# S4's convolution over 8 blocks of 256 samples, by the transforms of even and odd samples, in a kernel that runs it beside eight dense experts

## The chip, the cores and the metric

One core of one Trainium2 chip runs the whole kernel. The metric is the device time of one execution in microseconds, the median of three runs. TensorE multiplies matrices, VectorE and ScalarE work on elements, GpSimd (POOL) issues the accumulating DMAs here, and SyncE (SP) issues nearly all other DMAs, in the order in which the program lists them.

## The reference

For u of 2048 tokens and 512 channels, with xn the layer norm of u, the output is the sum of three branches:

```
xn  = layernorm(u)
out = u + A(xn) + B(xn)
A:  K[d, l] = Re sum_n C[d, n] * exp(dt[d] * A[d, n] * l) * dt[d] * B[d, n]      l = 0 .. 2047, n = 0 .. 127
    y[l, d] = sum_j K[d, j] * xn[l - j, d] + xn[l, d] * Dskip[d]                  (by FFTs of length 4096)
B:  sum over all 8 experts e of softmax(xn @ w_gate)[e] * (silu(xn @ w1[e]) @ w2[e])      w1: 512 x 1792, w2: 1792 x 512
```

All eight experts take part for every token, so branch B is dense. Branch A is called S4 here.

## The kernel before, in words

**The experts.** The outer loops run over 8 experts e, 4 blocks tb of 512 tokens and 4 groups d of w1's rows (two pairs of 128 each in the first three groups, one pair in the last). Every fp32 operand is split into a high and a low fp16 half, and a product is three matmuls. `product` (line 1371) makes the first layer into three PSUM tiles hb by seven products instead of eight (a Strassen-like scheme whose sums of weights and of tokens, w1s and xop, are made beforehand), in matmuls of 256 columns. `pop` (lines 1354 to 1356) makes the second layer y in matmuls of 512 columns. `block` lists it in four slots per group: a product, a copy between hb's tiles on ScalarE (lines 1605, 1615, 1600), activations (1387, 1391), then `slot`, which pops some units of the second layer, splits weights of the next expert, and lets S4 go on. The low half of an activation is made on VectorE (1400). The token sums xop are loaded anew for each block (line 1596, SP). The first block (`plain`, line 1662) is made without the scheme, while the inputs come in.

**S4.** It goes by 32 chunks c of 16 channels. Its state basis is made for two chunks at once (`s4_basis`). `s4_tables` makes powers by doubling on VectorE. `s4_kernel` contracts them on TensorE to K (kgen, 64 fp32 matmuls), and `s4_kernel_out` copies that to ksb on ScalarE and turns it through DRAM (kd) into kt, 128 positions by 16 blocks for each channel. `s4_kf` and `s4_uf` transform the blocks of K and of xn: 128-point transforms at half-odd frequencies as matmuls with dfth, 6 of 256 columns each. `s4_conv` then makes, frequency by frequency, the convolution over the 16 blocks as a complex product in three real ones, m = 0 to 15, on VectorE (lines 884, 889, 890), with its sums in lines 869 to 874, 897, 898. `s4_back` transforms back (yp, 6 matmuls of 256 columns) and `s4_out` scales into ysb and stores to ys4. All S4 results on TensorE, the transposes and the scale totals share one PSUM bank, tag "s4": `take_bank` evacuates what is there before the next takes it.

**What sets the order.** The order of each engine's instructions is written out when the program is made, by a planner. `bg_run`, once per slot, lets S4's VectorE steps go on as far as a budget allows, 0.92 of TensorE's time in the slot less VectorE's other work, by the modelled cost that each step yields. S4's products are one per slot at most: `s4_pe` lists for each c, in this order, kf(c), back(c-1), kernel(c+2), uf(c+1), each when `until` says that its operands' step was listed two slots before and the bank is free. `s4_dve(c)` lists the tables of c+2 and then the conv of c. Before the last block, `bg_until("s4")` lists what is left of S4; in that block `s4_final` adds ys4 to the output.

**Buffers that the steps below name.** ksb and ysb have one buffer each; kt one; s4raw two; the tables' temporaries are ta and tt. `load_rest` (lines 144 to 148) puts four small loads on SP's queue ahead of the next weights (493) and of the stores of xn to DRAM (`x0_send`, 307).

Of the kernel before, what the change touches and what calls it, by code (L numbers as in the profile page):

```python
# [18 lines left out]
P = 128  # L19
# [7 lines left out]
MULTS = (1, 128, 2, 256, 4, 512, 8, 1024, 16, 32, 64)  # L27
NK = len(MULTS)
XSH = 8
# [4 lines left out]
def s4_moe_kernel(  # L34
# [29 lines left out]
    NI = NT  # L64
    DQS = [(0, 1), (2, 3), (4, 5), (6,)]
# [318 lines left out]
    def gates_squares(row):  # L384
        gsq = sb.tile([P, KT * E], F32, tag="s4p1", bufs=1, name="gsq")
        S.activation(gsq, wgt.rearrange("p k e -> p (k e)"), AF.Square, accum_out=row)

    def gates_split():
# [3 lines left out]
        wgf = sb.tile([P, 6, E], F32, tag="s4p2", bufs=1, name="wgf")  # L392
# [265 lines left out]
    ZSH = 18  # L658

    def s4_dft_load():  # L660
        s4["dft"] = sb.tile([P, 4, P], F32, tag="tb", name="dft", bufs=1)
        nc.sync.dma_start(s4["dft"], dft)

    def s4_dft():

        dftt = s4["dft"]
        times(dftt[:, 2:4, :], dftt[:, 2:4, :], DSH)
        V.tensor_copy(dfth[:, 0], dftt)
        V.tensor_tensor(dfth[:, 1], dftt, dfth[:, 0], op=ALU.subtract)
# [6 lines left out]
    upad = cp.tile([P, 2, DC, NI + 1], F32, name="upad")  # L676
# [4 lines left out]
    def s4_raw(g):  # L681
        raw = sb.tile([P, 6, GD], F32, tag="s4raw", name=f"s4raw{g}", bufs=2)
        nc.sync.dma_start(raw, s4p[g])
        s4["raw", g] = raw

    def s4_basis(g):
# [20 lines left out]
        n4 = [P, 2, NK, DC]  # L707
# [8 lines left out]
        x = sb.tile(n4, F32, tag="b2", name=f"bx{g}", bufs=1)  # L716
# [25 lines left out]
        s4["basis", g] = (wv, zr, zi)  # L742
        yield 2 * tt_(352) + 0.3

    def s4_tables(c):
# [6 lines left out]
        for st in range(6):  # L752
# [9 lines left out]
            n4 = [P, 2, nn, L]  # L762
            zrv = zr[:, h, k0:k0 + ns, :].rearrange("p k d -> p (k d)").unsqueeze(1).unsqueeze(3).to_broadcast(n4)
            ziv = zi[:, :, h, k0:k0 + ns, :].rearrange("p c k d -> p c (k d)").unsqueeze(3).to_broadcast(n4)
            ta = sb.tile([P, 1024], F32, tag="ta", name=f"ta{c}_{st}", bufs=1)[:, :2 * nn * L]
            ta = ta.rearrange("p (c n l) -> p c n l", c=2, n=nn)
            tt = sb.tile([P, 1024], F32, tag="tt", name=f"tt{c}_{st}", bufs=1)[:, :2 * nn * L]
            tt = tt.rearrange("p (c n l) -> p c n l", c=2, n=nn)
            V.tensor_tensor(ta, tin, zrv, op=ALU.mult)  # L769
            if st > 2:  # L770
                yield tt_(2 * nn * L)
            V.tensor_tensor(tt, tin[:, ::-1], ziv, op=ALU.mult)
            if st > 2:
                yield tt_(2 * nn * L)
            V.tensor_tensor(tout, ta, tt, op=ALU.add)  # L775
            yield (1 if st > 2 else 3) * tt_(2 * nn * L) + 0.5 * (st == 0)
# [15 lines left out]
    def s4_kernel_out(c):  # L792
# [6 lines left out]
        kt = sb.tile([P, DC, NI], F32, tag="kt", name=f"kt{c}", bufs=1)  # L799
# [7 lines left out]
    def s4_kscale(c):  # L807


        ks = s4["ks", c] = sb.tile([P, 2], F32, tag="ksc", name=f"ksc{c}", bufs=4)  # L810
        pow2_scale(ks[:, 0:1], s4["kst", c], f"k{c}")
        pow2_inverse(ks[:, 1:2], ks[:, 0:1], ZSH - DSH)

# [10 lines left out]
    def s4_uload(c):  # L824

        uc = sb.tile([P, NI, DC], F32, tag="uc", name=f"uc{c}", bufs=1)
        nc.sync.dma_start(uc, xnd[:, :, c * DC:(c + 1) * DC])
        s4["uc", c] = uc.rearrange("p i d -> p d i")

    def s4_uhigh(c):  # L830
        uh = s4["uh", c] = sb.tile([P, 2, DC, NI], F16, tag="uh", name=f"uh{c}", bufs=1)
        S.copy(uh[:, 0], s4["uc", c])
        clock["act"] += at_(256)
# [4 lines left out]

    def s4_uf(c):
        uh = s4["uh", c]  # L840
        take_bank()
        uf = ps_s.tile([P, 2, DC, NI], F32, tag="s4", name=f"uf{c}")
        for a in range(2):
            for n, (x, y) in enumerate(((0, 0), (1, 0), (0, 1))):
                T.matmul(uf[:, a].rearrange("p d i -> p (d i)"), dfth[:, x, a, :], uh[:, y].rearrange("p d i -> p (d i)"),  # L845
                         start=(n == 0), stop=(n == 2))
        clock["pe"] += 0.66
# [4 lines left out]
    def s4_kf(c):  # L852
        take_bank()
        kf = ps_s.tile([P, 2, DC, NI], F32, tag="s4", name=f"kf{c}")
        kh = s4["kh", c]
        for a in range(2):
            for n, (x, y) in enumerate(((0, 0), (1, 0), (0, 1))):
                T.matmul(kf[:, a].rearrange("p d i -> p (d i)"), dfth[:, x, 1 - a, :], kh[:, y], start=(n == 0), stop=(n == 2))  # L858
        clock["pe"] += 0.66
        k4 = sb.tile([P, 4, DC, NI], F32, tag="k4", name=f"k4{c}", bufs=1)  # L860
        S.copy(k4[:, 0:2].rearrange("p a d i -> p (a d i)"), kf.rearrange("p a d i -> p (a d i)"))
        bank["at"] = now()
        s4["k4", c] = k4

    def s4_conv(c):

        up, k4 = upad, s4["k4", c]
        v3 = sb.tile([P, 3, DC, NI], F32, tag="v3", name=f"v3{c}", bufs=1)
        V.scalar_tensor_tensor(v3[:, 2], up[:, 1, :, 0:NI], sgnt[:, 1:2], up[:, 0, :, 1:], op0=ALU.mult, op1=ALU.add)
        V.scalar_tensor_tensor(v3[:, 1], up[:, 0, :, 0:NI], sgnt[:, 0:1], up[:, 1, :, 1:], op0=ALU.mult, op1=ALU.add)  # L870
# [4 lines left out]
        cost = 2 * tt_(256)  # L875
        s3 = sb.tile([P, 1024], F32, tag="ta", name=f"s3{c}", bufs=1)[:, :3 * DC * NI]
        s3 = s3.rearrange("p (n i) -> p n i", n=3 * DC)
        k3f = k4[:, 1:4].rearrange("p a d m -> p (a d) m")
        v3f = v3.rearrange("p a d m -> p (a d) m")
        for m in range(NI):  # L880
            n = NI - m
            kb = k3f[:, :, m:m + 1].to_broadcast([P, 3 * DC, n])
            if m == 0:
                V.tensor_tensor(s3, v3f, kb, op=ALU.mult)
                cost += tt_(768)
            else:
                tm = sb.tile([P, 1024], F32, tag="tt", name=f"tm{c}_{m}", bufs=1)[:, :3 * DC * n]
                tm = tm.rearrange("p (a i) -> p a i", a=3 * DC)
                V.tensor_tensor(tm, v3f[:, :, 0:n], kb, op=ALU.mult)  # L889
                V.tensor_tensor(s3[:, :, m:], s3[:, :, m:], tm, op=ALU.add)  # L890
                cost += 2 * tt_(48 * n)
            if m < 8 or m in (9, 11, 15):
                yield cost
                cost = 0.0
        z = sb.tile([P, 3, DC * NI], F32, tag="v3", name=f"z{c}", bufs=1)[:, 0:2]
        s3a = s3.rearrange("p (a d) i -> p a (d i)", a=3)
        V.tensor_tensor(z[:, 0], s3a[:, 0], s3a[:, 1], op=ALU.subtract)
        V.tensor_tensor(z[:, 1], s3a[:, 0], s3a[:, 2], op=ALU.add)
# [12 lines left out]
    def s4_back(c):  # L911
        zh = s4["zh", c]
        take_bank(lambda: s4_out(c))
        yp = ps_s.tile([P, DC, NI], F32, tag="s4", name=f"yp{c}")
        n = 0
        for a in range(2):
            for x, y in ((0, 0), (1, 0), (0, 1)):
                T.matmul(yp.rearrange("p d i -> p (d i)"), dfth[:, x, 2 + a, :], zh[:, y, a], start=(n == 0), stop=(n == 5))  # L918
                n += 1
        s4["yp", c] = yp  # L920
        clock["pe"] += 0.66

    def s4_out(c):
        ysb = sb.tile([P, NI, DC], F32, tag="ysb", name=f"ysb{c}", bufs=1)
        S.activation(ysb, s4["yp", c].rearrange("p d i -> p i d"), AF.Copy, scale=s4["ks", c][:, 1:2])
        nc.sync.dma_start(ys4[:, :, c * DC:(c + 1) * DC], ysb)
# [56 lines left out]
    def s4_pe():  # L983


        for c in range(-2, NCH + 1):
            if 0 <= c < NCH:
                if c:
                    yield from until(("z at", c - 1))
                yield from until(("kl", c))  # L990
                yield from bank_wait()
                s4_kf(c)
                s4["kf", c] = now()
                yield None
            if c > 0:
                yield from until(("zl", c - 1))
                yield from bank_wait()
                s4_back(c - 1)
                s4["back", c - 1] = now()
                yield None  # L1000
            if c + 2 < NCH:
                yield from until(("tab", c + 2))
                if c > -2:
                    yield from until(("kl", c + 1), more=-1)
                yield from bank_wait()
                s4_kernel(c + 2)
                s4["kn", c + 2] = now()
                polled.append(s4_ksplit(c + 2))
                yield None
                yield from bank_wait()  # L1010
                yield from until(("ke", c + 2))
# [763 lines left out]
```

## Time and profile before

| | us |
|---|---|
| median of three runs | 2327.32 (2326.92 to 2327.40) |
| profiled execution, first to last instruction (span) | 2325.2 |
| TensorE busy | 2312.5 |
| VectorE busy | 1961.5 |
| ScalarE busy | 1464.8 |
| GpSimd busy | 341.3 |

The profile gives the profiled execution's span alone; its own time is not listed apart, and the median stands 2.1 us above the span. Busy times are the union of an engine's recorded instructions; the ends of matmuls are modelled, so their spacing is read from starts. An idle time in brackets in a timeline is that of the engine ahead of the instruction, with what ended it.

### The profile page before, as it was taken

How to read it: one execution, taken by the hardware profiler on the slowest of the kernel's cores; microseconds unless marked ns; L12 is line 12 of the kernel's file. 1: busy time of each engine (PE TensorE's matmuls, PEld its weight loads, DVE VectorE, ACT ScalarE, POOL GpSimd, SP SyncE). 2: the span in 40 equal slices, each digit the busy share in tenths (PEclk: the TensorE clock that was granted, in tenths of full speed). 3: DMA queues.
4: the chain of work that ended last, by engine and by line, in shares of the span. 5: the costliest groups of instructions: out<-in, count | busy, mean ns of one | idle time of the engine just before them, and what ended most of it. 6: DMA issues, size and time to landing. Idle time of an engine off the chain costs nothing.

```text
span 2325.2 us, 45209 instructions
## 1 busy us (share of the span) xinstructions
PE 2312.5 (99%) x17701; PEld 1539.0 (66%) x17701; DVE 1961.5 (84%) x3810; ACT 1464.8 (63%) x2584; POOL 341.3 (15%) x395
## 2 busy tenths in 40 slices
PE   8999999999999999999999999999999999999999
PEld 4666666666666666666666666666666666666665
DVE  8854877989998999999899979999889997998611
ACT  7676665657666576665766657666576665764443
POOL 0000101121111111111111111111111110111112
PEclk9999999999999999999999999999999999999999
DMA  7696456575566655645556546564565654543447
GB/s 281 191 269 186 121 138 147 130 157 129 128 155 153 144 134 127 153 106 112 146 113 147 117 110 150 124 140 105 117 155 112 145 128 93 150 95 61 83 88 177
DMA packets 327686, 320.72 MB, mean 138 GB/s; under 512 B 183664, under 2 KB 220016, under 8 KB 327024
## 3 DMA queue, kind: packets, MB, share of 16 engines
q1 hardware_dynamic: 271024, 223.70, 31.7%
q0 software_dynamic: 55872, 93.61, 25.6%
q8 instruction: 138, 2.26, 0.4%
q14 instruction: 76, 0.62, 0.1%
q10 hardware_dynamic: 576, 0.52, 0.1%
HBM read 202.14 MB, written 66.06 MB: 115 GB/s over the span
## 4 chain that ended last, share of the span: by engine, by line
PE 98%; DMA 1%; DVE 0%; ACT 0%; SPq 0%; issue 0%; DVEq 0%; ACTq 0%
PE hb L1371 43%; PE y L1355 17%; PE y L1356 17%; PE y L1354 17%; PE kgen L787 1%; PE kf L858 1%; PE yp L918 1%; PE uf L845 1%; PE hb L1662 1%; PE tp L288 0%; DMA ut<-in_u_dram 0%; DMA w2s<-in_w_dram 0%; DMA xnd<-xn 0%; DMA f<-in_w_dram 0%; DMA ut0b<-in_u_dram 0%; DMA raw<-in_w_dram 0%
## 5 line engine op out<-in xcount | busy, mean ns | idle before, releaser
L1371 PE MATMUL hb<-xop,w1s 128*128 128x256 f16 x9114 | 1072.8, 273 | 0.0
L1371 PEld LDWEIGHTS <-w1s 128*128 128x128 f16 x9114 | 885.4, 98 | 173.3 <-issue 0.8
L1355 PE MATMUL y<-w2s,ahl 128*128 128x512 f16 x1792 | 679.2, 379 | 0.6 <-DVE w2s L509 0.6
L1356 PE MATMUL y<-w2s,ahl 128*128 128x512 f16 x1792 | 679.2, 379 | 0.0
L1354 PE MATMUL y<-w2s,ahl 128*128 128x512 f16 x1792 | 679.2, 379 | 0.0
L1356 PEld LDWEIGHTS <-ahl 128*128 128x128 f16 x1792 | 175.3, 98 | 212.2 <-issue 0.9
L1571 POOL DMA_DIRECT2D scC<-sE x124 | 118.2, 953 | 1266.2 <-ACT sE L1600 1082.6
L890 DVE TENSOR_TENSOR s<-s,tm 128x720 f32<-128x720 f32 (+14 forms) x480 | 268.9, 560 | 16.6
L1354 PEld LDWEIGHTS <-ahl 128*128 128x128 f16 x1792 | 175.3, 98 | 161.5
L1355 PEld LDWEIGHTS <-ahl 128*128 128x128 f16 x1792 | 175.3, 98 | 161.3
L1387 ACT ACTIVATE fa<-hb,sc 128x512 f32<-128x512 f32 (+1 forms) x252 | 160.4, 637 | 189.2 <-PE hb L1371 188.7
L889 DVE TENSOR_TENSOR tm<-v,k 128x720 f32<-128x720 f32 (+14 forms) x480 | 267.5, 557 | 10.7
L1400 DVE SCALAR_TENSOR_TENSOR ahl<-fa,sc,ahl 128x512 f16<-128x512 f32 (+1 forms) x262 | 178.7, 682 | 63.4 <-ACT ahl L1391 63.1
L1615 ACT COPY hb<-hb 128x512 f32<-128x512 f32 x124 | 64.1, 517 | 229.7 <-PE hb L1371 229.4
L1391 ACT ACTIVATE ahl<-fa,sc 128x512 f16<-128x512 f32 (+1 forms) x262 | 175.8, 671 | 9.8 <-DMA xnd<-xn 0.9
L1571 POOL DMA_DIRECT2D scB<-sE x124 | 107.1, 864 | 437.9 <-ACT scB L1600 324.0
L1605 ACT COPY hb<-hb 128x512 f32<-128x512 f32 x124 | 64.3, 519 | 168.3 <-PE hb L1371 167.7
L1400 DVE SCALAR_TENSOR_TENSOR ahl<-scB,sc,ahl 128x512 f16<-128x512 f32 x124 | 84.4, 680 | 77.4 <-ACT ahl L1391 76.0
L1400 DVE SCALAR_TENSOR_TENSOR ahl<-scC,sc,ahl 128x512 f16<-128x512 f32 x124 | 84.2, 679 | 67.6 <-ACT ahl L1391 64.0
L775 DVE TENSOR_TENSOR tb<-ta,tt 128x64 f32<-128x64 f32 (+2 forms) x192 | 131.9, 687 | 5.5
L769 DVE TENSOR_TENSOR ta<-tb,zr 128x64 f32<-128x64 f32 (+2 forms) x192 | 131.6, 686 | 5.4
L1332 POOL DMA_DIRECT2D oacc<-ye x108 | 95.9, 1334 | 244.7 <-ACT ye L1328 243.1
(252 smaller groups left out, 2447.2 us busy)
## 6 DMA issues: line engine op xcount, KB each, us to landing
xop<-xd SPq DMA_DIRECT2D x210, 256.0 KB, 3.8
pp<-in_w_dram SPq DMA_DIRECT2D x98, 512.0 KB, 4.4
raw<-in_w_dram SPq DMA_DIRECT2D x56, 512.0 KB, 4.8
oacc<-ye POOLq DMA_DIRECT2D x108, 256.0 KB, 6.2
scC<-sE POOLq DMA_DIRECT2D x93, 256.0 KB, 4.2
scB<-sE POOLq DMA_DIRECT2D x93, 256.0 KB, 4.2
raw<-in_w_dram SPq DMA_DIRECT2D x52, 256.0 KB, 4.2
raw<-in_w_dram SPq DMA_DIRECT2D x104, 128.0 KB, 4.1
```

Of the source, the lines that this page charges most:

```text
L769: V.tensor_tensor(ta, tin, zrv, op=ALU.mult)
L775: V.tensor_tensor(tout, ta, tt, op=ALU.add)
L889: V.tensor_tensor(tm, v3f[:, :, 0:n], kb, op=ALU.mult)
L890: V.tensor_tensor(s3[:, :, m:], s3[:, :, m:], tm, op=ALU.add)
L1354: T.matmul(y, lhs[0], w2s[pr][:, 0, fh, :], start=(c == 0), stop=False)
L1355: T.matmul(y, lhs[0], w2s[pr][:, 1, fh, :], start=False, stop=False)
L1356: T.matmul(y, lhs[1], w2s[pr][:, 0, fh, :], start=False, stop=(c == NF - 1))
L1371: T.matmul(dst[:, q, :], w1s[pr][:, a, wo, k * P:(k + 1) * P], xop[:, xo, b, k, :], start=(first_mm and q == 0 and n == 0), stop=(n == 5), ...
L1387: S.activation(fa, src[:, :n], AF.Silu, scale=w1_unscale(e, d if whole else prs[0]))
L1391: S.activation(ahl[:, 0, :n], fa, AF.Copy, scale=scales[e][:, 3:4])
L1400: V.scalar_tensor_tensor(ahl[:, 1, :n], fa, sc[:, 3:4], ahl[:, 0, :n], op0=ALU.mult, op1=ALU.subtract)
L1571: nc.gpsimd.dma_start(dst, src, accum_op=ALU.add)
```

## The change

S4's sequence is cut into 8 blocks of 256 samples instead of 16 of 128. A block's 256-point transform is made from two 128-point ones, of its even and of its odd samples, and a butterfly of two (sum and difference) on VectorE; the odd samples' matrix is turned by cos and sin of pi (2k + 1) / 512, which come with `mult`. So each of uf, kf and back has 12 matmuls of 128 columns, and the sum over blocks runs over m = 0 to 7 with twice the rows. The tables write their products into the output tile and add in place, their long stages in halves, with one temporary pt. uc and ys go by even and odd samples and by halves of the partitions, four DMAs instead of one. Buffers: ysb takes the tag of ksb, kt has two, s4raw one, the temporaries of `s4_basis` go into x. The multipliers are listed in another order, and mult_t comes in two DMAs. `s4_pe` no longer has a fixed order: in each slot it takes the first ready one of the next kernel, kf, back and uf. The tables, the conv chunks and the bases run as three lists side by side.

The core of the diff:

```diff
-MULTS = (1, 128, 2, 256, 4, 512, 8, 1024, 16, 32, 64)
+POWERS = (2, 256, 4, 512, 8, 1024, 16, 1, 32, 64)
+MULTS = (POWERS + (0, 128) + tuple(math.cos(math.pi * (2 * k + 1) / 512) for k in range(128))
+         + tuple(math.sin(math.pi * (2 * k + 1) / 512) for k in range(128)))
...
-        nc.sync.dma_start(mult_t, mult)
+        nc.sync.dma_start(mult_t[:, :, 0:NP - 1], mult[:, :, 0:NP - 1])
+        nc.sync.dma_start(mult_t[:, :, NP - 1:NP], mult[:, :, NP:NP + 1])
...
-        raw = sb.tile([P, 6, GD], F32, tag="s4raw", name=f"s4raw{g}", bufs=2)
+        raw = sb.tile([P, 6, GD], F32, tag="s4raw", name=f"s4raw{g}", bufs=1)
...
+            half = nn // 2 if st > 3 else nn
...
+                V.tensor_tensor(pt, tin[:, ::-1, r], ziv, op=ALU.mult)
+                V.tensor_tensor(tout[:, :, r], tin[:, :, r], zrv, op=ALU.mult)
...
+                V.tensor_tensor(tout[:, :, r], tout[:, :, r], pt, op=ALU.add)
...
-        kt = sb.tile([P, DC, NI], F32, tag="kt", name=f"kt{c}", bufs=1)
+        kt = sb.tile([P, DC, NI], F32, tag="kt", name=f"kt{c}", bufs=2)
...
-        nc.sync.dma_start(uc, xnd[:, :, c * DC:(c + 1) * DC])
+        for h in range(2):
+            for a in range(2):
+                nc.sync.dma_start(uc[64 * h:64 * h + 64, :, a], xnd[a::2, h::2, c * DC:(c + 1) * DC])
...
+    def transform(dst, src, row):
+
+
+        dst = dst.rearrange("p a (o d) i -> p a o d i", o=2)
+        for a in range(2):
+            for o in range(2):
+                for n, (x, y) in enumerate(((0, 0), (1, 0), (0, 1))):
+                    T.matmul(dst[:, a, o], dfth[:, x, 4 * o + row(a), :], src[:, y, o], start=(n == 0), stop=(n == 2))
...
+        transform(uf, uh, lambda a: a)
...
+        transform(kf, s4["kh", c].rearrange("p x (d o i) -> p x o d i", o=2, i=NB2), lambda a: 1 - a)
...
+    def butterfly(dst, src):
+        V.tensor_tensor(dst[:, :, 0:DC], src[:, :, 0:DC], src[:, :, DC:], op=ALU.add)
+        V.tensor_tensor(dst[:, :, DC:], src[:, :, 0:DC], src[:, :, DC:], op=ALU.subtract)
...
+        butterfly(v3[:, 1:3], vt)
...
+        butterfly(k4[:, 0:2], k4[:, 2:4])
...
-        for m in range(NI):
-            n = NI - m
-            kb = k3f[:, :, m:m + 1].to_broadcast([P, 3 * DC, n])
+        for m in range(NB2):
+            n = NB2 - m
+            kb = k3f[:, :, m:m + 1].to_broadcast([P, 6 * DC, n])
...
-        ysb = sb.tile([P, NI, DC], F32, tag="ysb", name=f"ysb{c}", bufs=1)
...
+        ysb = sb.tile([P, NB2, 2, DC], F32, tag="ksb", name=f"ysb{c}", bufs=1)
...
+        for h in range(2):
+            for a in range(2):
+                nc.sync.dma_start(ys4[a::2, h::2, c * DC:(c + 1) * DC], ysb[64 * h:64 * h + 64, :, a])
...
+        left = [
+            (kernel, list(range(NCH)), lambda c: at_least(1, "tab", c) and (c < 2 or at_least(-1, "kl", c - 2))),
+            (kf, list(range(NCH)), lambda c: at_least(1, "kl", c) and (c == 0 or at_least(1, "z at", c - 1))),
+            (back, list(range(NCH)), lambda c: at_least(1, "zl", c)),
+            (uf, list(range(NCH)), lambda c: at_least(1, "ul", c) and (c == 0 or at_least(1, "v3", c - 1))),
+        ]
+        while any(cs for _, cs, _ in left):
+            it = next((x for x in left if x[1] and x[2](x[1][0])), None)
+            if it is None or not bank_free():
+                yield None
+                continue
+            c = it[1].pop(0)
+            it[0](c)
+            yield None
+            if it[0] is kernel:
                 yield from bank_wait()
...
+                yield from until(("ke", c))
...
+        yield from together([chunks(), s4_tabs(), bases()])
```

## Rows read from the trace of the kernel before

**Rows 1.** The page: the span, busy time of three engines (us, share of the span, instructions), and TensorE's granted clock in 40 slices (9 is 90% or more of full speed).

```profile
span 2325.2 us, 45209 instructions
...
PE 2312.5 (99%) x17701; PEld 1539.0 (66%) x17701; DVE 1961.5 (84%) x3810; ACT 1464.8 (63%) x2584; POOL 341.3 (15%) x395
...
PEclk9999999999999999999999999999999999999999
```

**Rows 2.** The chain that ended last, followed back from the last instruction: shares of the span by line (the view cuts the line at its end).

```profile
by line: PE hb L1371 43.0%; PE y L1355 16.6%; PE y L1356 16.6%; PE y L1354 16.6%; PE kgen L787 1.4%; PE kf L858 0.9%; PE uf L845 0.9%; PE yp L918 0.9%; PE hb L1662 0.6%; PE tp L288 0.4%; DMA ut<-in_u_dram 0.4%; DMA w2s<-in_w_dram 0.3%; DMA 
```

**Rows 3.** Who waited for whom, TensorE's own waits, all of them: us in total, times, longest.

```profile
PE tot_a L178 <- DVE row L1178: 6.9, 1, 6.9
PE hb L1164 <- POOL ident masks.py:199: 1.4, 1, 1.4
PE y L1355 <- DVE w2s L509: 0.6, 1, 0.6
```

**Rows 4.** Stretches of the span: us, then busy us (instructions) of PE, PEld, DVE, ACT, POOL, the granted clock, DMA share, GB/s.

```profile
0.00:50.00 50.00, 41.13 (x235) 22.98 (x236) 42.09 (x106) 37.76 (x66) 2.34 (x7) 0.93 0.87 309
...
500.00:1000.00 500.00, 500.00 (x3881) 335.42 (x3880) 474.93 (x895) 320.14 (x568) 82.44 (x94) 1.00 0.61 138
...
1500.00:2000.00 500.00, 500.00 (x3878) 335.10 (x3877) 448.17 (x873) 313.62 (x573) 72.65 (x84) 1.00 0.55 125
```

**Rows 5.** Timeline of TensorE at three places (start, us, what, count): the gates' products at 121 us, eight transposes at 151 us, a kf transform at 373 us, each with the product that follows it.

```profile
121.48 0.24 PE L414 MATMUL lg<-wgs,xop 128*128 128x16 f16 x4
121.59 0.24 PE L417 MATMUL lg<-wgs,xop 128*128 128x8 f16 x4
...
151.42 0.61 PE L288 MATMUL tp<-ident,xl 128*128 128x128 f16 x8
151.87 0.38 PE L1354 MATMUL y<-w2s,ahl 128*128 128x512 f16 x1
...
373.89 0.82 PE L858 MATMUL kf<-kh,dfth 128*128 128x256 f16 x6
374.55 1.69 PE L1371 MATMUL hb<-xop,w1s 128*128 128x256 f16 x14
```

**Rows 6.** Line 858, the transforms kf: weight loads and products, count, duration in ns (min/median/max), first and last start in us. Lines 845 and 918 have the same counts.

```profile
L858 PEld LDWEIGHTS <-dfth x192: 97/98/98, 373.7 to 2172.6; 128*128 128x128 f16 x192
L858 PE MATMUL kf<-kh,dfth x192: 272/273/273, 373.9 to 2172.7; 128*128 128x256 f16 x192
```

**Rows 7.** VectorE: the two groups of the sum over m from the page's list of the costliest groups (out<-in, count | busy us, mean ns | idle before), then single shapes from the groups by shape.

```profile
L890 DVE TENSOR_TENSOR s<-s,tm 128x720 f32<-128x720 f32 (+14 forms) x480 | 268.9, 560 | 16.6
L889 DVE TENSOR_TENSOR tm<-v,k 128x720 f32<-128x720 f32 (+14 forms) x480 | 267.5, 557 | 10.7
...
L890 DVE TENSOR_TENSOR s<-s,tm 128x672 f32<-128x672 f32 x32 | 27.4, 858 | 1.1
L890 DVE TENSOR_TENSOR s<-s,tm 128x96 f32<-128x96 f32 x32 | 8.3, 259 | 1.1
L871 DVE TENSOR_TENSOR v<-v 128x256 f32<-128x256 f32 x32 | 13.6, 425 | 1.1
L769 DVE TENSOR_TENSOR ta<-tb,zr 128x1024 f32<-128x1024 f32 x64 | 78.2, 1222 | 1.6
L769 DVE TENSOR_TENSOR ta<-tb,zr 128x512 f32<-128x512 f32 x32 | 22.1, 690 | 1.0
```

**Rows 8.** First and last start of S4's kgen (line 787), of its last transform yp (line 918), and of the additions of its output in the last block (line 1554, GpSimd); columns as in rows 6.

```profile
L787 PE MATMUL kgen<-tb x2048: 219/219/243, 310.4 to 2115.3; 128*32 128x64 f32 x187
L918 PE MATMUL yp<-zh,dfth x192: 272/273/273, 431.1 to 2227.4; 128*128 128x256 f16 x192
L1554 POOL DMA_DIRECT2D oacc<-ys x16: 824/1341/2812, 2237.9 to 2296.0; - x16
```

**Rows 9.** Timeline of SP's queue in the first block: start and duration of the issues.

```profile
25.68 0.33 SPq L146 DMA_DIRECT2D sgnt<-in_sgn_dram  x1
26.95 0.33 SPq L147 DMA_DIRECT2D mult_t<-in_mult_dram  x1
28.27 0.33 SPq L148 DMA_DIRECT2D dt_all<-in_log_dt_dram  x1
29.01 0.97 SPq L493 DMA_DIRECT2D raw<-in_w_dram  x2
30.28 0.98 SPq L307 DMA_DIRECT2D xnd<-xn  x2
```

**Rows 10.** The chain that ended last, from 28 us: the landing of xnd's store (start, us); then the timelines of ScalarE and of TensorE behind it.

```profile
30.28 6.06 DMA xnd<-xn
...
36.42 0.72 ACT L1391 ACTIVATE ahl<-fa,sc 128x512 f16<-128x512 f32 x1 [0.93 <-DMA xnd<-xn]
...
39.55 0.38 PE L1355 MATMUL y<-w2s,ahl 128*128 128x512 f16 x1 [0.57 <-DVE w2s L509]
```

**Rows 11.** Timelines of ScalarE and of SP's queue where ksb follows ysb closest.

```profile
1291.54 0.45 ACT L925 ACTIVATE ysb<-yp,ksc 128x256 f32<-128x256 f32 x1
1296.45 0.39 ACT L795 ACTIVATE ksb<-kgen 128x256 f32<-128x256 f32 x1
1298.13 0.47 ACT L1387 ACTIVATE fa<-hb,sc 128x256 f32<-128x256 f32 x1 [0.79 <-PE hb L1371]
...
1292.02 0.57 SPq L926 DMA_DIRECT2D ys<-ysb  x1
1292.70 3.79 SPq L1596 DMA_DIRECT2D xop<-xd  x4
1297.36 0.32 SPq L801 DMA_DIRECT2D kd<-ksb  x1
```

**Rows 12.** Line 926, the store of ysb: from issue to landing, 32 DMAs.

```profile
DMA to landing us min/median/max: 3.2/4.7/11.3
```

**Rows 13.** ScalarE's copy ahead of the product that most often follows it (line 1615), from the page: count | busy us, mean ns | idle before it, and what ended that.

```profile
L1615 ACT COPY hb<-hb 128x512 f32<-128x512 f32 x124 | 64.1, 517 | 229.7 <-PE hb L1371 229.4
```

More of the change, by code (lines that the diff above doesn't have):

```diff
@@ L674, in s4_dt @@
         yield from exp_dve(dt_all, dt_all, *xx)
-    upad = cp.tile([P, 2, DC, NI + 1], F32, name="upad")
+    upad = cp.tile([P, 2, 2 * DC, NB2 + 1], F32, name="upad")
     V.memset(upad, 0.0)
@@ L742, in s4_basis @@
         s4["basis", g] = (wv, zr, zi)
+        s4["basis at", g] = now()
         yield 2 * tt_(352) + 0.3
@@ L841, in s4_uf @@
         take_bank()
[L842 to L847, printed above, removed]
+        uf = ps_s.tile([P, 2, 2 * DC, NB2], F32, tag="s4", name=f"uf{c}")
+        transform(uf, uh, lambda a: a)
         S.activation(upad[:, :, :, 1:].rearrange("p a d i -> p (a d) i"), uf.rearrange("p a d i -> p (a d) i"),
@@ L853, in s4_kf @@
         take_bank()
[L854 to L861, printed above, removed]
+        kf = ps_s.tile([P, 2, 2 * DC, NB2], F32, tag="s4", name=f"kf{c}")
@@ L983, in s4_pe @@
     def s4_pe():
[L986 to L990, printed above, removed]
-                yield from bank_wait()
[L992 to L1011, printed above, removed]
-            if 0 <= c + 1 < NCH:
-                if c >= 0:
-                    yield from until(("v3", c))
-                yield from until(("ul", c + 1))
-                yield from bank_wait()
-                s4_uf(c + 1)
-                s4["uf", c + 1] = now()
-                yield None
@@ new lines, in at_least, with kernel, kf, back @@
+        def at_least(more, *key):
+            return key in s4 and now() > s4[key] + more
+        def kernel(c):
+            s4_kernel(c)
+            s4["kn", c] = now()
+            polled.append(s4_ksplit(c))
+        def kf(c):
+            s4_kf(c)
+            s4["kf", c] = now()
+        def back(c):
+            s4_back(c)
+            s4["back", c] = now()
+        def uf(c):
+            s4_uf(c)
+            s4["uf", c] = now()
+        left = [
[4 more added lines that the diff above has]
+        ]
@@ L1057, in s4_dve @@
     def s4_dve(c):
-        if c + 2 < NCH:
-            if c > -2:
-                yield from until(("kn", c + 1), more=0)
-            yield from s4_tables(c + 2)
-            s4["tab", c + 2] = now()
         if c >= 0:
-            yield from until(("kf", c), more=0)
+            yield from until(("kf", c), ("uf", c), more=0)
             if c:
@@ L1073, in s4_dve, with s4_tabs @@
             polled.append(s4_zsplit(c))
+    def s4_tabs():
+        for c in range(NCH):
+            if c:
+                yield from until(("kn", c - 1), more=0)
+            yield from until(("basis at", c // 2), more=-1)
+            yield from s4_tables(c)
+            s4["tab", c] = now()
     def s4_x(c):
@@ L1101, in s4_all, with chunks, bases @@
         polled.append(s4_pe())
-        for c in range(-2, NCH):
-            gens = [s4_dve(c)]
-            if 0 <= c + 1 < NCH:
-                gens.append(s4_x(c + 1))
-            if c % 2 and c + 3 < NCH:
-                gens.append(s4_next((c + 3) // 2))
-            yield from together(gens)
+        def chunks():
+            for c in range(-1, NCH):
+                gens = [s4_dve(c)]
+                if c + 1 < NCH:
+                    gens.append(s4_x(c + 1))
+                yield from together(gens)
+        def bases():
+            for g in range(1, NCH // 2):
+                yield from s4_next(g)
+        yield from together([chunks(), s4_tabs(), bases()])
     ctx.enter_context(tc.manual_schedule())
```

131 lines of the change are left out of this document (72 added, 59 removed).

## The prediction

> **What bounds the kernel now.** I read the page's busy times first, then the chain that ended last, then who TensorE waits for, then its busy time by stretch. TensorE is busy 2312.5 of 2325.2 us at the full granted clock, VectorE 1961.5 [rows 1]. In the chain hb has 43.0% and the three lines of y 16.6% each; what follows is S4: kgen 1.4%, and kf, uf and yp 0.9% each [rows 2]. TensorE's recorded waits are 6.9, 1.4 and 0.6 us [rows 3]; they fill the 8.87 us that the first 50 us lack, and after that the stretches show it busy all the time, 500.00 of 500.00 us, while VectorE stands at 474.93 and later at 448.17 [rows 4]. "Busy" is modelled, so I checked it by starts: the six kf products of 256 columns begin at 373.89 and the next product at 374.55, so 0.66 us for six, 109 ns each [rows 5], as wide as their stream and with nothing between. The reader is to see that no engine but TensorE sets the end, that VectorE is nearly full but never late, and that therefore only two things can move the time: TensorE's own work, and a new wait that reaches TensorE.
>
> **The change, part by part.**
>
> *S4's transforms on TensorE.* Three sets (uf, kf, yp) of 6 products x 32 chunks, 192 of each [rows 6], become 12 products of 128 columns instead of 6 of 256. The columns stay: 6 x 256 = 12 x 128 = 1536. What is added is the fixed part of 6 more products. The price of a 128-column product with a weight load of its own stands in the trace: eight transposes start at 151.42 and the next product at 151.87, 0.45 us / 8 = 56 ns [rows 5]. The gates' products, on the same 128*128 of the array, follow each other at 0.11 us / 4 = 27 ns [rows 5], so the 98 ns of a weight load [rows 6] is a latency that runs ahead, not a spacing. So 12 x 0.45 / 8 = 0.675 us against 0.66: 0.015 us a transform, and x 96 = **+1.4 us** (the rows' rounding leaves some 1.5 us either way), all on the path since TensorE has no idle time to hide it. Bounds: 0, and above, if each such product had to wait out its own weight load, 12 x 98 - 6 x 109 = 0.52 us, x 96 = +50 us. I take the transposes' value, the same shape and type. One thing has no row: kf's moving operand is now read in runs of 8 halves with gaps; I take it as free, and if its 12 products took twice 56 ns, it would be 0.67 x 32 = +21 us.
> By the Trainium skill (TensorE: Matmul & The Clock Gate, Back-to-back issue gap), pairs of a weight load and a 128-column product sustain about 81 ns in a real kernel. The transposes' 56 ns speaks against it; by the page the term would be (12 x 81 - 6 x 109) ns x 96 = +30 us.
>
> *kgen* keeps its 2048 products, and `tot` its 32: nothing.
>
> *VectorE.* The sum over m goes from 15 multiply-add pairs on 48 rows to 7 on 96: 268.9 + 267.5 us [rows 7] become, by the forms of 672 down to 96 elements (858 down to 259 ns, evenly spaced, mean 558 ns), 2 x 7 x 558 ns x 32 = 250 us, so -286. Six butterfly operations of 256 elements at 425 ns [rows 7] x 32 add 82. The tables' two long stages, 3 x 1222 ns each, become 6 x 690 ns each: (4140 - 3666) x 64 = +30. In sum **-174 us on VectorE** (1961 to some 1785), and nothing on the path: VectorE waits for others, and TensorE waits for it only at the start, 6.9 and 0.6 us [rows 3]. This cover works the other way too: if an operation in place cost more than its row, up to these 174 us are there to absorb it. What VectorE's gain triggers: S4 comes earlier. Its last yp starts at 2227.4 and the last block's first addition of S4's output at 2237.9 [rows 8]; with S4 the rest of a full VectorE, the last yp should move to between 1980 and 2180. TensorE does the same products in another order, so the end does not move.
>
> *Order by readiness.* A product is still queued at least two slots after its operands' step and one per slot, so each still finds its data. VectorE's conv(c) now may start one slot after uf(c) was queued: it waits for ScalarE's copy to upad, and the next block's low parts stand behind it on VectorE. That pattern is there before with kf, and no y product waited for it. I put 0, and up to 1 us.
>
> *Loads ahead of the first blocks.* `mult_t` takes two DMAs in place of one on SP's queue, ahead of dt_all, of raw and of the four sends of xn. SP issues there at one per 1.3 us (sgnt 25.68, mult_t 26.95, dt_all 28.27), and the first send of xn goes at 30.28 [rows 9]; it lands 6.06 us later, ScalarE idles 0.93 us for it, and 3 us on TensorE idles 0.57 [rows 10]. That is a path with no slack. One more issue moves the send by up to 1.3 us; but if the landing is set by the bytes queued ahead, which hardly grow, by about nothing. I take the middle, **+0.6 us**, bounds 0 and 1.3.
>
> *DMAs on SP.* uc and ys go as four DMAs of 64 partitions each instead of one: 6 more issues a chunk at 0.3 to 0.57 us [rows 11], at most 3.4 us of SP per chunk of 60 us. Behind them stand the reloads of xop, as the four that follow ys at 1292.70 [rows 11]: up to 1.7 us later, for data needed a whole short block, about 10 us, later. I put 0. s4raw with one buffer makes SP wait for VectorE before its 16 loads; as uc does today. 0.
>
> *ysb takes ksb's buffer.* New waits: ScalarE may write ksb only when ys has landed, and ysb only when kd has landed. At 1291.54 ScalarE writes ysb, SP sends it at 1292.02, and at 1296.45 ScalarE writes ksb [rows 11]. ys lands 3.2 to 11.3 us after its issue, median 4.7 [rows 12]. With three more issues ahead of the last quarter (1.0 to 1.7 us) this ksb would start between 0 and 2 us later; behind it on ScalarE stands the activation of hb, which had 0.79 us idle before it [rows 11], and TensorE needs the copies of hb some products later. On average ScalarE stands idle 230 / 124 = 1.85 us ahead of such a copy [rows 13]. So a wait of 2 us is mostly absorbed. I take **+0.5 us** in all, bounds 0 and the rival below.
>
> **Sum.** 1.4 + 0.6 + 0.5 = +2.5 us on the profiled 2325.2, so a span of 2327.7. The runs' median of 2327.32 lies 2.1 us above the span; I forecast 2327.3 + 2.5 = **2329.8 us**, no measurable change (0.2% is 4.65 us: 2322.7 to 2332.0, about what a measurement of this kernel can tell).
>
> **The rivals.**
> - *ScalarE held by the shared buffer* (slower). Products picked by readiness put a kgen two slots behind a yp in every chunk, not now and then; then ksb waits for ys. The case above, at a median landing, costs up to 2 - 0.8 = 1.2 us; a landing of 11 us costs 4 or more. With half of the chunks so: 16 x 1.2 = 19 us, 2349. It decides where the distance from ysb to ksb falls below some 6 us plus ScalarE's idle time; for it speaks the 4.9 us from start to start at 1291.54, against it ScalarE's idle time.
> - *A 128-column product costs its weight load or its broken reads* (slower). 20 to 50 us: 2350 to 2380. Against it the transposes and gates [rows 5]. By the page of the Trainium skill above it would be 2358 (2327.3 + 30 + 1).
> - *S4 late* (slower). The last block waits until S4 is through. If conv, kf and kgen now wait for each other in turn and a chunk takes longer than today's (2227 - 310) / 32 = 60 us (first kgen 310.4 [rows 8]), the 10 us between last yp and last block are lost at once, and a chunk left over costs its conv, (250 + 82) / 32 = 10 us, and the hops from product to copy to split around it, as much again by my estimate: some 20 us, 2350. Against it VectorE's 174 us.
> - *VectorE's relief reaches TensorE* (faster). It would need over 7 us of TensorE waits that VectorE's work on S4 causes (4.65 and the 2.5 of the sum); behind the first 50 us the trace has none [rows 4].
> - *The change doesn't save what it says*: VectorE's butterflies and split tables eat the gain. Time as forecast.
>
> **How the numbers follow.** No measurable change, 2327.3 to 2332.0: 0.80 (the last rival within it). Shared buffer 0.11, weight load or reads 0.04, S4 late 0.03: slower 0.18. Faster 0.02. The range of 8 in 10 starts at 2327.0, where no term of the sum is more than nothing, and reaches to 2335.0, where the startup is at its bound and the shared buffer costs some 5 us; above it stay the rest of that rival and the two others.
>
> **What would show it.** In the changed profile: uf, kf and yp with 384 products each at 56 ns from start to start; no wait of TensorE after the first 40 us; its wait for w2s there at 0.6 to 1.9 us; VectorE near 1785 us; the last yp before 2180. ksb's line on ScalarE with a wait for ys is the first rival's mark, each such wait with a late hb copy. The forecast is wrong if the twelve products take more than 0.7 us, if ScalarE's waits for ys sum to over 10 us, or if TensorE has gaps within the blocks.

## The result, and the profile after

The changed kernel takes **2339.47 us** (median of four runs, 2335.49 to 2341.60) against 2327.15 for the kernel before beside it: a ratio of 1.0051 over all runs, interval 1.0038 to 1.0064. It is slower by 0.5%, and the forecast of 2329.8 (2327.0 to 2335.0) is too low. Its runs spread over 6 us, those of the kernel before over 0.5. The profiled run took 2341.54 us, so its rows show the upper end of the four; its span is 14.6 us over the 2325.2 of [rows 1].

The page of the changed kernel, span and busy times, to hold against [rows 1]:

```profile
span 2339.8 us, 46590 instructions
...
PE 2318.6 (99%) x18277; PEld 1548.9 (66%) x18277; DVE 1767.7 (76%) x3686; ACT 1471.9 (63%) x2584; POOL 340.3 (15%) x395
```

VectorE lost 194 us as the change says, and the span grew. TensorE's busy time grew by 6.1 us and the time outside it by 8.5 (21.2 against 12.7). So the next view is who TensorE waits for, to hold against [rows 3]: all its waits but one of 0.2 us, then one of VectorE and the waits of ScalarE that matter below (total us, times, longest). The names in them: scB, scC and sE are ScalarE's copies of hb; tot_k and tot_w are scale totals that TensorE makes in S4's bank, and st_k is ScalarE's copy of the first out of it; zi and zr are the sines of S4's basis and bf their argument, made on VectorE; base is a block of u's tokens, loaded for the output; ye is y, copied out of PSUM.

```profile
PE tot_a L183 <- DVE row L1220: 7.3, 1, 7.3
PE hb L1413 <- ACT scC L1642: 4.0, 3, 1.3
PE tot_w L183 <- ACT st_k L178: 3.2, 1, 3.2
PE hb L1206 <- POOL ident masks.py:199: 1.4, 1, 1.4
PE kgen L800 <- DVE tb L788: 1.3, 1, 1.3
...
DVE xs L1353 <- DMA base<-in_u_dram: 24.5, 3, 13.5
ACT zi L738 <- DVE bf L735: 11.2, 2, 8.8
ACT ksb L808 <- DMA ys<-ysb: 4.5, 5, 2.1
ACT ysb L955 <- DMA ys<-ysb: 0.4, 1, 0.4
```

The first and fourth rows are the startup, as before. New are five waits within the blocks: three of hb for a copy by ScalarE, one of tot_w for ScalarE, one of kgen for VectorE. None is for ys or uc, the DMAs that I had looked at. The stretches say where they lie, columns as in [rows 4]; the last row is a finer stretch:

```profile
500.00:1000.00 500.00, 498.67 (x4102) 337.01 (x4101) 462.44 (x957) 326.29 (x581) 83.10 (x95) 1.00 0.63 140
1000.00:1500.00 500.00, 497.34 (x4169) 337.04 (x4168) 452.71 (x960) 323.39 (x582) 67.82 (x78) 1.00 0.55 122
1500.00:2000.00 500.00, 498.67 (x4042) 336.96 (x4041) 374.10 (x779) 315.07 (x568) 73.14 (x84) 1.00 0.56 125
...
431.60:437.40 5.80, 5.75 (x25) 3.27 (x25) 5.59 (x9) 4.00 (x9) 2.56 (x3) 0.50 0.77 130
```

Where [rows 4] had 500.00 of 500.00, TensorE now lacks 1.33, 2.66 and 1.33 us; and behind the longest gap it ran at a granted clock of 0.50, the lower of its two levels, until 437.4. TensorE's timeline at four places:

```profile
360.52 0.83 PE L861 MATMUL kf<-kh,dfth 128*128 128x128 f16 x12
361.19 1.47 PE L1413 MATMUL hb<-xop,w1s 128*128 128x256 f16 x12
...
427.76 0.38 PE L1398 MATMUL y<-w2s,ahl 128*128 128x512 f16 x1
431.33 0.16 PE L183 MATMUL tot_w<-r,ones 128*128 128x1 bf16 x1 [3.19 <-ACT st_k L178]
431.65 2.72 PE L1413 MATMUL hb<-xop,w1s 128*128 128x256 f16 x12 [0.17 <-ACT hb L1647]
434.17 0.63 PE L1396 MATMUL y<-w2s,ahl 128*128 128x512 f16 x1
434.60 0.63 PE L1397 MATMUL y<-w2s,ahl 128*128 128x512 f16 x1
...
728.56 0.30 PE L800 MATMUL kgen<-tb 128*32 128x64 f32 x4
730.12 1.09 PE L800 MATMUL kgen<-tb 128*32 128x64 f32 x60 [1.25 <-DVE tb L788]
...
1137.48 0.38 PE L1398 MATMUL y<-w2s,ahl 128*128 128x512 f16 x1
1139.19 2.78 PE L1413 MATMUL hb<-xop,w1s 128*128 128x256 f16 x24 [1.33 <-ACT scC L1642]
```

Starts are read here, not the modelled ends: y products follow each other at 0.22 us at full clock, so the gap at 431 is 431.33 - 427.76 - 0.22 = 3.35 us, the one at 1139 is 1139.19 - 1137.48 - 0.22 = 1.49 us; two more of 1.49 lie at 1433.19 and 1727.19, in the same slot of the next two experts. At half clock the twelve hb products take 2.52 us from start to start and y 0.43, twice their usual.

The third place is kgen, which starts four of its 64 products and then waits for the tables tb that VectorE is still writing: 1.47 us by starts, from 728.64, where the fourth starts.

Why ScalarE was late stands in the timelines of SP, VectorE and ScalarE ahead of 431 us, and of ScalarE ahead of 1139 us:

```profile
407.63 1.06 SPq L814 DMA_DIRECT2D kd<-ksb  x1
413.20 1.75 SPq L816 DMA_DIRECT2D kt<-kd  x4
415.05 0.86 SPq L1347 DMA_DIRECT2D base<-in_u_dram  x2
...
418.92 0.55 DVE L1353 TENSOR_SCALAR xs<-base,mean,rstd 128x512 f32<-128x512 f32 x1 [13.53 <-DMA base<-in_u_dram]
...
427.39 0.34 DVE L735 TENSOR_SCALAR bf<-bf 128x352 f32<-128x352 f32 x1
...
427.77 0.50 ACT L738 ACTIVATE zi<-bf 128x352 f32<-128x352 f32 x1 [8.79 <-DVE bf L735]
...
430.65 0.56 ACT L1642 COPY scB<-hb 128x512 f32<-128x512 f32 x1
431.11 0.16 ACT L178 COPY st_k<-tot_k 128x1 f32<-128x1 f32 x1
...
1133.30 2.40 ACT L1370 ACTIVATE ye<-y,gse 128x512 f32<-128x512 f32 x4
1135.58 0.51 ACT L738 ACTIVATE zi<-bf 128x352 f32<-128x352 f32 x1
1136.12 0.50 ACT L739 ACTIVATE bf<-bf 128x352 f32<-128x352 f32 x1
1136.65 0.59 ACT L740 ACTIVATE zr<-bf,halfpi 128x352 f32<-128x352 f32 x1
1137.14 1.13 ACT L511 ACTIVATE w1s<-tw,sc 128x1024 f16<-128x1024 f32 x1
1138.18 0.49 ACT L829 ACTIVATE kh<-kt,ksc 128x256 f16<-128x256 f32 x1
1138.58 0.56 ACT L1642 COPY scC<-hb 128x512 f32<-128x512 f32 x1
```

Read the first part downwards. SP issues kd by 408.7 and then waits at kt until kd has landed (413.2). The loads of base stand behind kt on SP's queue and land late. VectorE, whose instructions run in the order of its list, idles 13.53 us for base, and bf, an S4 step behind that in its list, ends only at 427.7. ScalarE waits 8.79 us for it at the sine zi; behind the sines stand the copy of hb and the copy st_k that frees S4's bank, and TensorE waits for these. The second part has no wait at all. ScalarE is given one after the other the evacuation of y (2.40), the two sines and the absolute value between them (1.6), a split of weights (1.13) and kh (0.49), and the copy of hb that TensorE needs comes behind all of them.

The account against the span: 3.35 and, between tot_w and hb, 0.30 at 431, 1.47 at 730, 3 x 1.49, together 9.6 us of gaps. 434.60 - 434.17 against 0.22 says that the 6.1 us of work from 431.3 to 437.4 ran at half clock, which lost 3 us. The transforms add 1.4: by starts a set of uf, kf or yp takes 0.670 us in this trace and 0.655 in that of before (medians of the 96 sets). That is 14.0 of the 14.6.

### The profile page after: what moved, and what is told of

It is laid out like the page before. It is cut to its first block, busy times and chain, and to the rows that moved or that the text cites. A ratio compares the mean times of both kernels' runs of the same rounds, so it can differ in the third digit from the quotient of the medians.

```text
span 2339.8 us, 46590 instructions
## 1 busy us (share of the span) xinstructions
PE 2318.6 (99%) x18277; PEld 1548.9 (66%) x18277; DVE 1767.7 (76%) x3686; ACT 1471.9 (63%) x2584; POOL 340.3 (15%) x395
## 4 chain that ended last, share of the span: by engine, by line
PE 94%; DMA 2%; ACT 2%; DVE 1%; SPq 1%; issue 0%; DVEq 0%; ACTq 0%
PE hb L1413 41%; PE y L1397 16%; PE y L1398 16%; PE y L1396 16%; PE kgen L800 1%; PE uf L861 1%; PE kf L861 1%; PE yp L947 1%; PE hb L1704 1%; PE tp L293 0%; ACT ye L1370 0%; DMA w2s<-in_w_dram 0%; SPq L958 0%; DMA base<-in_u_dram 0%; DMA dsk<-in_dskip_dram 0%; ACT ahl L1433 0%
## 5 line engine op out<-in xcount | busy, mean ns | idle before, releaser
L788 DVE TENSOR_TENSOR tb<-tb,pt 128x512 f32<-128x512 f32 (+3 forms) x256 | 141.5, 553 | 5.2
L784 DVE TENSOR_TENSOR pt<-tb,zi 128x512 f32<-128x512 f32 (+3 forms) x256 | 141.2, 551 | 5.0
L785 DVE TENSOR_TENSOR tb<-tb,zr 128x512 f32<-128x512 f32 (+3 forms) x256 | 140.3, 548 | 0.0
L916 DVE TENSOR_TENSOR s<-s,tm 128x672 f32<-128x672 f32 (+6 forms) x224 | 127.8, 570 | 7.7
```

What stands on the lines that cost most here:

```text
L784: V.tensor_tensor(pt, tin[:, ::-1, r], ziv, op=ALU.mult)
L785: V.tensor_tensor(tout[:, :, r], tin[:, :, r], zrv, op=ALU.mult)
L788: V.tensor_tensor(tout[:, :, r], tout[:, :, r], pt, op=ALU.add)
```

## The experiments

Ratios are against the kernel before, run beside each, with 95% intervals.

**1. The transforms alone.** The kernel before, with each of its three transforms in 128-column products (here uf):

```diff
-                T.matmul(uf[:, a].rearrange("p d i -> p (d i)"), dfth[:, x, a, :], uh[:, y].rearrange("p d i -> p (d i)"),
...
+                for h in range(2):
+                    hd = slice(8 * h, 8 * h + 8)
+                    T.matmul(uf[:, a, hd].rearrange("p d i -> p (d i)"), dfth[:, x, a, :], uh[:, y, hd].rearrange("p d i -> p (d i)"),
...
```

> The kernel before, with each of its 6 transform products of 256 columns cut into two of 128, nothing else. If the products cost what the transposes showed (56 ns each), +1.4 us: 2328.6. If part of the 12 us comes from them (weight loads), more: 2333 or above.

Measured 2328.20 against 2327.53, 1.0004 [0.9995, 1.0013]. The products' number and width are not the cause. (The change's strided operands aren't in this run; the 0.670 us above has them in.)

**2. The DMAs alone.** The kernel before, with uc and ys in four DMAs each (here ys):

```diff
-        nc.sync.dma_start(ys4[:, :, c * DC:(c + 1) * DC], ysb)
+        for h in range(2):
+            for a in range(2):
+                nc.sync.dma_start(ys4[64 * h:64 * h + 64, 8 * a:8 * a + 8, c * DC:(c + 1) * DC], ysb[64 * h:64 * h + 64, 8 * a:8 * a + 8])
```

> The kernel before, with uc's load and ys's store as four DMAs each, of 64 partitions and 8 blocks, nothing else. Theory 'order' (the new order puts S4's steps beside other work of ScalarE and SP): no effect, 2327 to 2328. Rival 'queue' (SP, held by 6 more issues of 0.6 us a chunk, brings base, xop and kd late whatever the order): a good part of the 12 us, 2331 to 2338, with waits of TensorE for ScalarE in the trace.

Measured 2326.85 against 2327.53, 0.9998 [0.9989, 1.0007]. Under the lists of before, SP's queue has room for them.

**3. The old lists.** The changed kernel with the fixed order of S4's products and of its VectorE steps as before:

```diff
-        left = [
-            (kernel, list(range(NCH)), lambda c: at_least(1, "tab", c) and (c < 2 or at_least(-1, "kl", c - 2))),
...
+        for c in range(-2, NCH + 1):
+            if 0 <= c < NCH:
+                if c:
+                    yield from until(("z at", c - 1))
+                yield from until(("kl", c))
...
-        yield from together([chunks(), s4_tabs(), bases()])
+        for c in range(-2, NCH):
...
+            yield from together(gens)
...
```

> The changed kernel with the order of before: kf, back, kernel, uf in turn for each chunk, tables and conv of a chunk in one list. Eight blocks, twelve products, four DMAs and the shared buffer stay. Theory 'order': TensorE's waits behind the first 50 us go, 2328.5 to 2330.5. Rival 'queue': it stays at 2334 to 2341.

Measured 2342.66 against 2327.53, 1.0068 [1.0051, 1.0084]; my expectation missed. A wait of ScalarE, and TensorE's timeline near the end:

```profile
ACT zh L931 <- DVE z L884: 12.4, 2, 11.1
...
2238.37 0.38 PE L1397 MATMUL y<-w2s,ahl 128*128 128x512 f16 x1
2250.49 1.44 PE L947 MATMUL yp<-zh,dfth 128*128 128x128 f16 x12 [11.74 <-ACT ysb L955]
```

The waits within the blocks are gone but for one of 0.2 us, but S4 now comes too late: its last yp starts at 2251.6 where [rows 8] had 2227.4. The end of the blocks waits 11.9 us for it, while VectorE still makes the last conv (ScalarE waits 11.1 us for its z), and the granted clock is 0.50 from 2240.9 to 2254.5, so the first 4 us behind the gap run at half speed. Without the new lists the new convolution has no such gaps, and is late. Why it is late stays open. From 1000 to 1500 us VectorE was busy 402 of 500, so there at least VectorE is not what holds S4 up; the hops from engine to engine are a guess that no run tested.

**4. The sines not beside evacuations.** The changed kernel, with S4's sines kept out of slots in which ScalarE evacuates y:

```diff
-        if room > 1.0 and run_later():
+        if room > 1.0 and not clock["read"] and run_later():
```

> The changed kernel, but the basis' three sine activations are not listed in a slot in which ScalarE also evacuates y. Theory 'order': the three stalls of 1.49 us ahead of hb (1139, 1433, 1727 us) go, so 4.5 us less than the changed kernel in the same state, 2331 to 2337; the stall at 431 us may stay. If ScalarE's load there is not the sines' place but its sum, the stalls move elsewhere and the time stays at 2335 to 2341.

Measured 2333.02 against 2327.53, 1.0026 [1.0015, 1.0037]: 6.5 us better than the changed kernel. Two of TensorE's waits, and its last transform:

```profile
PE tot_w L183 <- ACT st_k L178: 2.4, 1, 2.4
PE kgen L800 <- DVE tb L788: 1.7, 1, 1.7
...
L947 PE MATMUL yp<-zh,dfth x384: 219/219/219, 432.8 to 1941.0; 128*128 128x128 f16 x192
```

The three gaps of 1.49 us are gone, at the same pace of S4 (last yp 1941.0, in the changed kernel 1949.2). The gap at 430 (2.6 us by starts) and kgen's remain. No half clock followed this time, so a part of the 6.5 us may come from that.

**5. The loads of base earlier**, on top of 4:

```diff
-            for n, f in ((7, base), (8 + j % 2, base_add), (11, base_send)):
+            for n, f in ((5, base), (8 + j % 2, base_add), (11, base_send)):
```

> As d_sines, and the loads of the tokens' base listed two slots earlier (5 in place of 7). Theory 'base': at 404 to 417 us VectorE stands 12.8 us for base, which SP lists behind kd and kt; so the sines are late, ScalarE stands behind them, and TensorE loses 2.9 us at 430. With the load earlier that stall goes: 330 ns of it may stay, 2330 to 2331. Rival 'full': VectorE is too full there, whatever it waits for; the stall stays or moves, 2332.5 to 2334.

Measured 2333.05 against 2327.18, 1.0027 [1.0016, 1.0037]: no gain. Who waited, and ScalarE's timeline:

```profile
DVE xs L1353 <- DMA base<-in_u_dram: 6.8, 4, 3.2
PE hb L1413 <- ACT hb L1647: 3.4, 1, 3.4
...
774.87 0.62 ACT L847 CAST uh<-uc 128x256 f16<-128x256 f32 x1 [6.99 <-DMA uc<-xnd]
```

VectorE's wait for base falls from 25.7 us (experiment 4) to 6.8 and the gap at 430 goes with it, as the chain said. But a new one opens at 776: ScalarE waits 6.99 us at another S4 step, uh, with a copy of hb behind it. TensorE loses 3.5 us by starts, and then runs at a granted clock of 0.50 until 779.2. One gap closed, the next one shows.

**6. S4 slower.** The changed kernel with a smaller share of TensorE's time as S4's budget on VectorE; then with the condition of 4 as well, and then with both edits of 5:

```diff
-    SHARE = 0.92
+    SHARE = 0.84
```

> The changed kernel with S4's budget cut from 0.92 to 0.84 of TensorE's time; the sines as in the changed kernel. Theory 'haste' (S4 takes VectorE's gain to be through 280 us early, and its steps pile up beside the other work): most stalls go, 2328 to 2332, with the last yp at 2050 to 2150. Rival 'place' (each stall comes from which steps meet in one slot): other steps meet, 2333 to 2341.

> As h_share, with the sines kept out of slots with evacuations as in d_sines. Theory 'haste': 2328 to 2330, TensorE's waits behind 50 us under 1 us. Rival 'place': 2330 to 2334, a stall of 1 to 3 us in one or two places.

> All three: sines out of slots with evacuations, base earlier, budget 0.84. If the three causes are all there is, TensorE has no wait behind 50 us and the twelve-column products' 1.4 us is left: 2328 to 2329.5. It does not beat the kernel before by theory, since TensorE's own work is 1.4 us more.

Measured 2329.39, 2329.30 and 2329.62 against 2327.18: 1.0010 [1.0000, 1.0020], 1.0010 [1.0000, 1.0019], 1.0009 [0.9999, 1.0018]. None can be told from the kernel before with certainty. With the share alone, one wait of 0.3 us within the blocks is left, and the last yp starts at 2165.2, nearer to the 2227.4 of before; the other edits then add nothing. The lists are the new ones here, so they make the gaps only together with a higher share.

**7. The dose.** The changed kernel with a share of 0.88 and of 1.0:

```diff
-    SHARE = 0.92
+    SHARE = 0.88
```

> The changed kernel with a budget of 0.88. Theory 'haste': between 2329.4 (0.84) and 2339 (0.92), 2330 to 2335, the last yp at about 2050. Rival 'place': no such order, anything from 2329 to 2341.

> The changed kernel with a budget of 1.0: S4 asks for all that TensorE's time leaves on VectorE. Theory 'haste': more and longer stalls, 2342 to 2370, the last yp before 1900. Rival 'place': other stalls, not more of them, 2333 to 2342.

Measured 2336.78 and 2356.19 against 2326.99, 1.0041 [1.0026, 1.0056] and 1.0125 [1.0110, 1.0140]. From 0.84 to 1.0 the medians go 2329.4, 2336.8, 2339.5, 2356.2, and the last yp starts at 2165.2, 2081.1, 1949.2 and 1882.9: in these four, the faster S4, the longer the whole. At 0.88 it came out above what I expected. TensorE's wait at 0.88, and the sine ahead of it on ScalarE's timeline:

```profile
PE tot_k L183 <- ACT ksb L809: 4.8, 1, 4.8
...
434.02 0.50 ACT L738 ACTIVATE zi<-bf 128x352 f32<-128x352 f32 x1 [5.55 <-DVE bf L735]
```

It is the same chain in the same place: VectorE idles 9.0 us for base, the sines come late, and behind them stands ScalarE's copy ksb, for which TensorE waits. On SP's queue base stands behind kt again, which waits for kd until 407.3, and here behind the four issues of uc too (3.5 us), so the cut DMAs have a part in it. This one gap of 5.0 us and the half clock behind it (2.4 us lost) are most of the 9.8 us; how long a kernel takes still depends on which steps meet, and four shares are few to draw a line through.

**8. The new lists with the old convolution.** The changed kernel with the 16 blocks of 128, the six products and the single DMAs of before put back; lists, tables and buffers stay new:

```diff
-        for m in range(NB2):
-            n = NB2 - m
-            kb = k3f[:, :, m:m + 1].to_broadcast([P, 6 * DC, n])
+        for m in range(NI):
+            n = NI - m
+            kb = k3f[:, :, m:m + 1].to_broadcast([P, 3 * DC, n])
...
```

> The changed kernel's lists (products by readiness, tables, chunks and bases side by side, tables in place, the shared buffer of ksb and ysb) round the convolution of before: 16 blocks, six products of 256 columns, one DMA each for uc and ys. Theory 'order' (the free lists at a budget of 0.92 let S4's steps fall late beside other work, whatever the convolution): stalls behind 50 us stay, 2330 to 2342. Rival 'eight blocks' (the stalls come with the shorter convolution or its four-piece DMAs): 2327 to 2328.5, no wait of TensorE behind 50 us.

Measured 2332.77 against 2326.99, 1.0023 [1.0013, 1.0033]. TensorE's new waits and that of the sine, then the last transform:

```profile
ACT zi L731 <- DVE bf L728: 2.8, 1, 2.8
PE hb L1401 <- ACT hb L1645: 1.8, 2, 1.6
PE hb L1401 <- ACT scC L1630: 1.5, 3, 1.0
...
L938 PE MATMUL yp<-zh,dfth x192: 272/273/273, 438.4 to 2216.3; 128*128 128x256 f16 x192
```

The gaps need neither the new convolution nor a faster S4: the last yp starts at 2216.3, 11 us ahead of [rows 8], and TensorE waits for ScalarE all the same, the longest time behind the sine at 430. With 3, which has the new convolution and the old lists and no such gap, this puts the gaps on the lists, at the share of 0.92 that both have. Tables and buffers are new in both, so whether the lists alone would do it is not shown.

**9. The sines later.** On top of 4, the sines are listed four slots behind VectorE's step instead of one, so that VectorE's lateness doesn't reach ScalarE:

```diff
-        act_later.append((clock["slot"] + 1, sines))
+        act_later.append((clock["slot"] + 4, sines))
```

> As d_sines (budget 0.92, sines not beside evacuations), with the sines listed four slots after VectorE's clamp of their argument instead of one, so that a late VectorE doesn't hold ScalarE. Theory 'ScalarE stands behind a sine that waits for VectorE': the stall at 430 us goes, the one of kgen at 726 us (1.9 us, tables late) may stay or move with the bases: 2328.5 to 2331. Rival 'haste alone' (any step of S4 will be late at this budget): another stall of 2 to 4 us takes its place, 2332 to 2335 as d_sines and e_base.

Measured 2328.82 against 2327.14, 1.0007 [0.9997, 1.0016], the lowest of all with the new convolution. The wait for base is still there, and TensorE's waits within the blocks are gone but for one:

```profile
DVE xs L1353 <- DMA base<-in_u_dram: 22.3, 5, 8.6
PE hb L1413 <- ACT scC L1642: 0.3, 1, 0.3
...
L947 PE MATMUL yp<-zh,dfth x384: 219/219/219, 428.5 to 2098.9; 128*128 128x128 f16 x192
```

The edit also slows S4 (last yp 2098.9), so a part of its gain could be the pace. Against that stands 0.88 in experiment 7: nearly the same pace (last yp 2081.1), and 8 us longer, though without the condition of 4.

## Why the prediction was wrong

**The step that failed** is "Order by readiness", where I put 0, and up to 1 us, because each product "still finds its data". For one kgen that is wrong: at 730 it is queued behind tables that VectorE has not finished, and TensorE loses 1.47 us. The larger part I had not followed at all: what stands behind S4's steps on the engines between. I priced the order of the products, and one pattern on VectorE; the three lists side by side, which let S4's bases, tables and conv run against each other, I gave no price. Their small steps reach VectorE and ScalarE in slots where the blocks need these engines. ScalarE works off its list in order: at 431 a sine that waits for VectorE, and at 1139 sines beside an evacuation, hold the copies of hb behind them. Shown by 3 (old lists: no such gap), 8 (new lists without the new convolution: gaps), 4 and 9 (only the place of the sines changed: the loss against the kernel before falls from 12.3 us to 5.5 and to 1.7). In the profiled run the step measured 9.6 us of gaps and 3 us of half clock, in place of my 0 to 1. Which of the lists does it, the picking of the products or the three lists side by side, was not separated, and at a share of 0.84 the same lists leave one wait of 0.3 us (6).

**VectorE's gain.** The size was right: 194 us off, predicted 174. "Nothing on the path" was right for a gain, but the sentence that S4 comes earlier was left without a price: the last yp moved to 1949.2, further than the 1980 to 2180 that I gave, and S4's work was packed into a shorter stretch. Experiments 6 and 7 show that at a lower share the same work takes less time. [rows 4] shows VectorE at 475 of 500 us with TensorE never waiting for it; I took from it that VectorE is never late; it may as well say that this order fitted.

**The transforms** were right: twelve products in 361.19 - 360.52 = 0.67 us, 56 ns each, with kf's operand read in short runs, against 0.66 us for six in [rows 5]. The 0.670 and 0.655 us over all sets make +1.4 us, as forecast, which lies within the interval of experiment 1. By the Trainium skill (TensorE: Matmul & The Clock Gate, Back-to-back issue gap) such pairs would sustain about 81 ns; the trace doesn't agree, and the measurement decides.

**The startup** (+0.6). The first send of xn goes at 31.23 instead of 30.28 [rows 9]; sgnt, ahead of the added issue, is already 0.33 us later, so the issue itself moves the send by 0.62, as I took. But y's wait for w2s [rows 3] is no longer among TensorE's waits. The wait for tot_a ahead of it was between 6.0 and 7.6 us in the profiles of the experiments, so a term of 0.6 us can't be told from that.

**The shared buffer** (+0.5). ScalarE waits 4.9 us in all for ys, below the mark of 10 that I had set, and none of TensorE's gaps stands behind one. Experiments 3, 6 and 9 keep the shared buffer; 9 comes within 1.7 us of before. **The DMAs on SP** by themselves cost nothing (experiment 2). SP's order matters in another way: base stands behind kt, which waits for kd, and at a share of 0.88 behind uc's four issues as well.

**The rivals.** "S4 late" is real under the old lists (experiment 3); the new lists prevent it, and at this share they pay with the gaps. That rival and the term I put at 0 were two sides of one choice. "Shared buffer", "weight load" and "VectorE's relief" did not happen. My last line named the mark that came true, "TensorE has gaps within the blocks", but no rival had a mechanism for it.

**Open:** why the runs of the changed kernel differ by 6 us was not traced. One reading is that the half clock behind the gap, worth 3 us, comes in some runs only: the two longer runs list a mean granted clock of 0.998 and 0.999, the two shorter 1.000. But runs of the kernel before differ as much in that figure and not in time, so it isn't shown. No version tried beats the kernel before: with the gaps gone, what is left is 1.4 us more work on TensorE, by its starts, and VectorE's gain is on an engine that sets no end. A ysb with a buffer of its own was not tried.

## What to carry to other kernels

When work in the background gets cheaper, or free to run when ready, follow each of its steps to the engine on which it is queued in order, and ask what the bottleneck needs from that engine behind it; pricing the products on the bottleneck itself is not enough. Try a lower pace for the background before mending single waits, because each mended wait can show the next. And an order in which a nearly full engine makes nobody wait may be a fitted one: a change of it can cost time, even where no work is added.

## What the runs showed of the hardware

- A gap of 3.35 us on TensorE that ended at 431.3 was followed by half clock until 437.4, which cost another 3 us; at a share of 0.88 the gap of 5 us that ended at 436.5 likewise (434.5 to 441.3 at 0.50), and in experiment 5 the one of 3.5 us (775.8 to 779.2). The gap of 2.6 us in experiment 4, and those of 1.5 us, were not followed by one. At a share of 1.0 a gap of 2.25 us that ended at 899.7 was (900.7 to 904.1), and one of 2.7 us at 516 was not, so the length of the gap alone did not decide it.
- SP took a median of 633 ns for each quarter of ys, against 566 ns for the whole one before, so the four quarters of a chunk took it some four times as long.
- ScalarE's write of ysb, by even and odd samples, took 716 ns against 475, for the same 256 elements a partition.
- VectorE's addition of the last step of the sum over m, 96 elements in runs of one, took 333 ns, against 259 ns for 96 in runs of two [rows 7]; at 672 elements both took 858.
